# One ring of seven PSUM banks with a new order in the attention, and an own order for its last quad

## The chip, the core and the metric

One core of a Trainium2 chip runs the whole block. Its engines are TensorE (PE, with weight loads PEld), VectorE (DVE), ScalarE (ACT), GpSimd (POOL) and SyncE (SP, which issues DMAs). The metric is device microseconds of one execution.

## The reference

A transformer block with adaptive layer norm. Attention has 32 heads of 18 dimensions and one key/value head for all of them; the MLP has 4608 hidden units. All tensors are float32; x is 2048 x 576.

```python
mod = (_silu(c) @ w_mod).reshape(c.shape[0], 6, 1, -1)
sa, ca, ga, sb, cb, gb = (mod[:, i] for i in range(6))
h = _layernorm(x, axis=-1) * (1 + ca) + sa
x = x + ga * _A_ref(h, A_wq, A_wk, A_wv, A_wo)
h = _layernorm(x, axis=-1) * (1 + cb) + sb
x = x + gb * _B_ref(h, B_w1, B_b1, B_w2, B_b2)

# _A_ref: multi-query attention
scores = jnp.einsum("bhqd,bkd->bhqk", q, k) * (Dh ** -0.5)
p = _softmax(scores, axis=-1)
o = jnp.einsum("bhqk,bkd->bhqd", p, v)
```

## The kernel before

Three stages follow one another. Stage 1 (to about 134 us) makes layer norm, projections and the first maxima. Stage 2 (134 to 1374 us) is the attention. Stage 3 is the MLP. Only stage 2 and its seam to stage 3 are touched.

**Quads.** The attention runs over 32 quads: four blocks of 512 queries (`tb`) by eight groups of four heads. In quad n the engine PE works through a written list of tokens: `QUAD` for n = 0 to 8, `QUADW` for n = 9 to 30, and a list built from `LAST` and `LASTW` for n = 31. PE executes in this order and cannot pass a waiting instruction.

- `S0`, `S1`: a score matmul (`st_mm`, L931): 128 keys by 512 queries of one head, contraction over 64 rows, row group 0 or 1 of the array. ACT takes its exp into a P tile (L933). A quad has 64. There are four P tiles (`bufs=4`), each for 128 keys (`kc`), so four score matmuls fill one.
- `M0`, `M1`: a maxima matmul for the next quad (L319): 128 queries by 512 keys. DVE reduces it to one maximum per query (L953). A quad has 48.
- `X1`, `R1`: eight pairs per quad that get the last two key blocks with one reduction: ACT takes the Relu of a matmul with key differences (L941, L944), and DVE combines it with a second matmul (L319, L951).
- `Vk`: P·V for k quarter blocks of 128 queries (`pv_mm`, L921), four heads side by side in column groups of 32. It lags 8 quarter blocks behind; a quad has 64. The sum of a quad stands in the bank `psC`.
- `WO`: one of 24 pieces of the output product (`wo_next`, L723), 14 matmuls of 288 columns for 128 rows of an earlier block, added to x by DVE (L727). In some quads it is followed by two transposes of a layer-norm tile (L155), which also take a bank each.
- `T1 RC T2 OS`: the rest of the quad before (`post_quad`): transpose on DVE (L741), reciprocal and product (L744, L745), transpose back (L747), and split into two parts `os` (L757, L758), which DMAs on SP put in place. `F1 F2` finish the maxima. `RW` reloads a part of the output weights.

**Banks.** PSUM has eight banks. Before, scores, X, WO and small products take the next of four banks `psB`, maxima the next of three `psM`, and `psC` has one. In quad 31, and at the end of quad 30, where no maxima are left, every second score takes a `psM`. A matmul waits until the engine that reads the bank's former content is done.

**Quad 30** has one more `WO` at its end. In **quad 31** the list gives a V4 after every four scores, and one `WO` in the middle.

**The seam.** After the last P·V, ACT copies `psC` to O. PE then runs `wo_tile(t, 0, KD - 1)` for tiles t = 0, 1, 2 of the last block (24 matmuls each), which needs nothing of the last quad, while ACT and DVE do the last `post_quad` with `form` steps for the MLP between (L1049, L1056, L1058; `todo`, L1082). Then `wo_tile(t, KD - 1, KD)` adds the last part to tiles 0 to 2, and tile 3 (`rest`) is done between the first MLP products. Tiles 0, 1 and 3 use `psA` (two buffers), tile 2 two `psB`.

Of the kernel before, what the change touches and what calls it, by code (L numbers as in the profile page):

```python
# [32 lines left out]
def block_kernel(ctx: ExitStack, tc, x, wqkv, wo, w1, b1, w2, b2, c, wmod, ident_in, out):  # L33
# [850 lines left out]
    QUAD = """S0 M0 S1 S1 M0 V3 S0 M1 S1 M0 M1 S0 V3 M0 S1 M1 S0 V2 M0 S1 S1 M0 X1 S0 V4 T1 X1 M0 M1 M0 S1 S0
            V4 S1 RC M0 S1 S0 M0 S0 M1 V3 S0 M1 R1 S1 S0 M0 X1 V3 M0 S1 S1 R1 S0 M0 S1 V3 M0 X1 M0 S0 S1 S0
            M1 V3 M0 S1 S1 M0 S0 R1 S0 V3 R1 S0 S1 M1 S0 M0 X1 V3 M0 S1 M0 S1 S0 S0 R1 V3 M0 X1 S0 M1 S0 M1
            V3 S1 M0 M0 S1 T2 S0 S1 V4 M0 S1 S0 M1 S0 M1 V3 S0 R1 S1 M0 F1 S1 S0 V3 X1 M0 S1 M0 R1 S0 F2 OS
            V4 M0 M1 S0 S1 M0 X1 V4 S1 M0 S1 S0 M1 M0 S1 V2 R1 S0 M1 S0 V2 S0 S1 M0 M1 V2 S1""".split()
# [616 lines left out]
```

## Time and profile before

| | us |
|---|---|
| median of 3 runs | 2227.75 |
| lowest, highest | 2227.24, 2228.18 |
| span of the profiled execution | 2225.7 |
| PE busy | 2207.4 |
| DVE busy | 1931.9 |
| ACT busy | 1639.8 |
| POOL busy | 1527.0 |

The span runs from the first to the last instruction of the profiled execution; the device time of a run has about 2 us around it. Busy time of PE counts a matmul from start to its modelled end, with waits of the pipeline in it. Where this document gives a time of day, it is in us from the start of that span. A quad is measured from one O copy (L738) to the next.

### The profile page before, as it was taken

How to read it: one execution, taken by the hardware profiler on the slowest of the kernel's cores; microseconds unless marked ns; L12 is line 12 of the kernel's file. 1: busy time of each engine (PE TensorE's matmuls, PEld its weight loads, DVE VectorE, ACT ScalarE, POOL GpSimd, SP SyncE). 2: the span in 40 equal slices, each digit the busy share in tenths (PEclk: the TensorE clock that was granted, in tenths of full speed). 3: DMA queues.
4: the chain of work that ended last, by engine and by line, in shares of the span. 5: the costliest groups of instructions: out<-in, count | busy, mean ns of one | idle time of the engine just before them, and what ended most of it. 6: DMA issues, size and time to landing. Idle time of an engine off the chain costs nothing.

```text
span 2225.7 us, 46108 instructions
## 1 busy us (share of the span) xinstructions
PE 2207.4 (99%) x16630; PEld 1451.2 (65%) x16630; DVE 1931.9 (87%) x3415; ACT 1639.8 (74%) x3145; POOL 1527.0 (69%) x1761
## 2 busy tenths in 40 slices
PE   8999999999999999999999999999999999999999
PEld 6654544444544445454454545888888898989898
DVE  7589999999999999999999983887888878888887
ACT  5569999999999999999999997444444444343443
POOL 6653455666776687677676631888888867877776
PEclk9999999999999999999999999999999999999999
DMA  6232143433333333333333322666666646676664
GB/s 231 85 131 92 34 135 115 139 125 119 127 119 114 115 129 105 107 126 111 126 123 117 115 70 63 205 178 175 178 179 180 185 129 182 180 218 188 177 185 124
DMA packets 184776, 308.00 MB, mean 138 GB/s; under 512 B 19711, under 2 KB 75407, under 8 KB 184549
## 3 DMA queue, kind: packets, MB, share of 16 engines
q1 hardware_dynamic: 184405, 304.91, 44.3%
q8 instruction: 132, 2.16, 0.4%
q14 instruction: 95, 0.78, 0.1%
q10 hardware_dynamic: 144, 0.15, 0.0%
HBM read 200.97 MB, written 93.79 MB: 132 GB/s over the span
## 4 chain that ended last, share of the span: by engine, by line
PE 93%; ACT 1%; DVE 1%; issue 0%; ACTq 0%; DVEq 0%
PE psC L921 24%; PE psB L1144 18%; PE psA L1247 16%; PE psB L931 14%; PE psM L319 12%; PE psB L723 2%; PE psB L941 2%; PE psA L1281 1%; PE psA L723 1%; ACT P L933 1%; PE psB L155 0%; PE psB L248 0%; PE psB L357 0%; PE psM L931 0%; DVE mx L344 0%; DVE mx L337 0%
## 5 line engine op out<-in xcount | busy, mean ns | idle before, releaser
L933 ACT ACTIVATE P<-psB 128x512 f32<-128x512 f32 x2008 | 1051.1, 621 | 43.8 <-PE psM L319 20.0
L953 DVE TENSOR_REDUCE mx<-psM 128x1 f32<-128x512 f32 x1476 | 934.3, 682 | 29.9 <-PE psM L319 12.9
L931 PE MATMUL psB<-qst,KS 64*128 64x512 f32 x2008 | 603.5, 435 | 0.1
L319 PE MATMUL psM<-KS,qst 64*128 64x512 f32 x1722 | 591.2, 435 | 0.5 <-DVE mx L337 0.5
L921 PE MATMUL psC<-P,V 128*32 128x256 f32 (+3 forms) x6600 | 571.9, 440 | 0.5 <-ACT O L738 0.5
L931 PEld LDWEIGHTS psB<-qst,KS 64*128 64x128 f32 x2008 | 300.4, 184 | 225.6 <-ACT P L933 185.1
L319 PEld LDWEIGHTS psM<-KS,qst 64*128 64x128 f32 x1722 | 284.1, 184 | 185.6 <-DVE mx L953 130.2
L1144 PE MATMUL psB<-ops,w1a 128*128 128x512 f32 x1512 | 393.8, 396 | 0.2 <-DVE h L1159 0.2
L1144 PEld LDWEIGHTS psB<-ops,w1a 128*128 128x128 f32 x1512 | 270.1, 188 | 46.7 <-DVE h L1159 0.6
L921 PEld LDWEIGHTS psC<-P,V 128*32 128x32 f32 x6600 | 146.4, 108 | 185.3 <-issue 156.6
L1253 DVE TENSOR_TENSOR XT<-psA,XT 128x576 f32<-128x576 f32 x330 | 241.8, 753 | 18.6 <-PE psA L1247 13.2
L1247 PEld LDWEIGHTS psA<-w2s,big 128*128 128x128 f32 x1584 | 223.0, 188 | 14.0 <-POOL big L1221 2.5
L1247 PE MATMUL psA<-w2s,big 128*128 128x288 f32 x1584 | 230.5, 294 | 0.0
L1157 ACT ACTIVATE psB<-gs 128x512 f32<-128x512 f32 x144 | 86.7, 602 | 127.8 <-DVE gs L1156 127.7
L1221 POOL TENSOR_TENSOR big<-s,big 128x512 fp32r<-128x512 f32 x132 | 170.8, 1294 | 10.6
L951 DVE CUSTOM_DVE_ANT_0 xc<-psM,xc 128x512 f32<-128x512 f32 x246 | 166.3, 683 | 12.8 <-PE psB L931 6.4
L1153 ACT ACTIVATE h<-psB,b1t 128x512 f32<-128x512 f32 x144 | 97.9, 680 | 102.0 <-PE psB L1144 81.3
L758 POOL TENSOR_TENSOR os<-O,os 128x512 fp32r<-128x512 f32 x31 | 39.9, 1286 | 185.4 <-ACT os L757 185.4
L944 ACT ACTIVATE xc<-psB 128x512 f32<-128x512 f32 x246 | 154.7, 629 | 4.0 <-PE psB L941 1.4
L1156 DVE SCALAR_TENSOR_TENSOR gs<-psB,h 128x512 f32<-128x512 f32 x144 | 98.6, 685 | 39.8 <-ACT psB L1154 39.7
L792 POOL TENSOR_TENSOR r<-r,r 128x256 fp32r<-128x256 f32 (+1 forms) x162 | 121.8, 752 | 13.0
L1162 ACT ACTIVATE big<-h 128x512 fp32r<-128x512 f32 x39 | 24.7, 634 | 133.8 <-DVE h L1159 133.8
(212 smaller groups left out, 3326.8 us busy)
## 6 DMA issues: line engine op xcount, KB each, us to landing
w1a<-w1scr SPq DMA_DIRECT2D x252, 256.0 KB
w2s<-w2sum SPq DMA_DIRECT2D x132, 288.0 KB
w1scr<-r SPq DMA_DIRECT2D x126, 256.0 KB
w2s<-w2scr SPq DMA_DIRECT2D x76, 288.0 KB
w2scr<-r SPq DMA_DIRECT2D x72, 288.0 KB
w2sum<-r SPq DMA_DIRECT2D x72, 288.0 KB
qst<-qscr SPq DMA_DIRECT2D x192, 72.0 KB
w1a<-w2scr SPq DMA_DIRECT2D x33, 288.0 KB
```

Of the source, the lines that this page charges most:

```text
L319: pe.matmul(o, QST[n][64 * g:64 * g + 64, p, 128 * qt:128 * (qt + 1)], KS[64 * g:64 * g + 64, 512 * kb:512 * (kb + 1)], start=True, stop=True)
L792: po.tensor_tensor(o[:, n:2 * n], src, o[:, :n].bitcast(F32), op=ALU.subtract)
L921: pe.matmul(PVt[n][32 * j:32 * (j + 1), cs], V[:, kc, :], t[:, j, cs], start=(kc == 0 and h0 == 0), stop=(kc == 15), skip_group_check=True)
L931: pe.matmul(t, KS[64 * g:64 * g + 64, 128 * kc:128 * (kc + 1)], QST[n][64 * g:64 * g + 64, i, :], start=True, stop=True)
L933: ac.activation(P[n, kc][:, 2 * i + g, :], t, AF.Exp, scale=SCALE)
L944: ac.activation(XC[-1], t, AF.Relu)
L951: ve.tensor_tensor_reduce(c, t, c, 1.0, -3.0e38, ALU.add, ALU.max, o)
L953: ve.tensor_reduce(o, t, axis=AX.X, op=ALU.max)
L1144: pe.matmul(o, x, y, start=(first and i == 0), stop=(i == len(terms) - 1), skip_group_check=True)
L1221: po.tensor_tensor(unit(u, 1), x, unit(u, 0).bitcast(F32), op=ALU.subtract)
L1247: pe.matmul(p[:, i, :288], x[:, ts_], W2S[k][:, y], start=(bool(first) and q == 0), stop=(q == 2), skip_group_check=True)
L1253: ve.tensor_tensor(o, p[:, :, :288], o, op=ALU.add)
```

## The change

The seven banks besides `psC` become one ring, from which each token takes the bank that was taken longest ago; each `+` behind a token skips one. All of the stage's users take from it. `QUAD` keeps its sequence and gets `+` marks; `QUADW` is a new sequence with marks. Quad 30 loses its extra `WO`. Quad 31 has a list of its own (`LAST`): P·V in runs of 8 to 12 quarter blocks, two `WO`, and two `WP`: the first 12 matmuls of the output product of tile 2 of the last block, one half each, added to x at once. So the seam runs only tiles 0 and 1 ahead, tile 2 starts at its last part (`first=KD - 1`), and the `form` steps stand behind most of the last `post_quad`.

```diff
-    def psB(): return PS["t"].tile([128, 512], F32, name="psB", bufs=PS["b"])
+    def psB(): return bank() if RING else PS["t"].tile([128, 512], F32, name="psB", bufs=PS["b"])
+    RING = []
+    def bank(rank=0):
+        b = RING.pop(rank)
+        RING.append(b)
+        return PS["t"].tile([128, 512], F32, name="bk%d" % b, bufs=1)
...
     open_ps("2", 4)
-    psM(), psC()
+    RING.extend(range(3))
+    bank(), bank(), bank(), psC()
+    RING[:] = 3, 0, 4, 1, 5, 2, 6
...
-    def wo_mm(tb, t, h2, p, k0, k1):
+    def wo_mm(tb, t, h2, p, k0, k1, end=KD, first=0):
...
-                pe.matmul(p[:, :288], a, b, start=(k == 0 and i == 0), stop=(k == KD - 1 and i == len(terms) - 1))
+                pe.matmul(p[:, :288], a, b, start=(k == first and i == 0), stop=(k == end - 1 and i == len(terms) - 1))
...
-    QUAD = """S0 M0 S1 S1 M0 V3 S0 M1 S1 M0 M1 S0 V3 M0 S1 M1 S0 V2 M0 S1 S1 M0 X1 S0 V4 T1 X1 M0 M1 M0 S1 S0
...
-    QUADW = """M1 M1 S0 S0 X1 S1 M0 V4 S1 M0 S1 S0 M1 M0 V4 M0 S1 S0 M0 S1 T1 M0 X1 V4 S1 RC S0 S0 M1 M0 S1 V4
-            S0 R1 M1 S0 S1 M0 S1 V3 S1 M0 S0 X1 M0 M0 S1 V2 M0 S1 S0 R1 V2 M0 X1 M0 S1 S0 S1 M0 V4 S0 T2 R1
-            M0 S1 OS S0 M1 WO S0 R1 M1 S0 M1 S0 X1 V3 S0 M1 M0 S1 S1 M1 S0 V3 M0 S1 S0 R1 S0 M0 X1 V3 M0 S1
-            X1 M0 S1 M0 S1 V4 S1 M0 R1 S0 M1 S0 V4 S0 M1 M0 F1 S1 S0 S1 V4 M0 S1 M0 X1 S0 M1 F2 V4 M1 S0 S0
-            S1 M0 S1 M0 V3 R1 S0 S0 S1 R1 M0 V3 S0 S1 M0 S1 M0 S1 V3 M0 S1 M1 S0 M1 S0 V3""".split()
-    LASTW = "S0 S1 S0 S1 S0 S1 WO V4 S0 S1 V4".split()
-    LAST = "S0 S1 S0 S1 V4 S0 S1 S0 S1 V4".split()
+    QUAD = """S0+ M0 S1 S1+ M0 V3 S0 M1 S1+ M0 M1++ S0 V3 M0 S1+ M1 S0+ V2 M0 S1+ S1 M0+ X1 S0+ V4 T1 X1 M0 M1 M0
...
+    QUADW = """S1+ M0 M0 X1 S0 X1 M0 V3 S1 M0 M0+ S1 R1 S0+ V2 M1 S0 M0 S1+ S0 R1+ V3 M0 X1+ S0 S1+ S0+ M1 V4 S0 T1
+            M1+ S0 S1 M0 S1+ V4 S1 M0 M1 S0 S1+ M0 V4 S1 M0 S1 S0+ M1 S0 R1 V4 S1 M0 M0 RC X1+ S0 M1+ S1 V3 S0
+            M1 S1+ S0 M0 S1 M0 V3 R1 S1 M0 M1+ S0 S1+ S0 V4 S1 T2 OS M0 X1++ M0 S1+ M0 WO S0 M1 S0 M1 S0 M1 V3
+            S1 S0 M1 S0 M0 X1 V3 S1 M0 M1+ M0 S1+ S0 V4 M0 S1+ S0 S1 S0+ R1+ M0 V4 S0+ S1 M0 M1++ M1 S0+ V3 S0
+            R1 M0+ F1 S1 S0 X1+ V4 M0 S1 M0 S1+ S0+ M1 F2 V3 S0+ R1 S0+ S1 M0 S1 M0 V3 M0 X1 S1 M0+ S1 R1+ S0 V3""".split()
+    LAST = """S1 S0 S1 S0 V8 S0 S1 T1 RC S0 S1 T2 S0 S1 WO S0 S1 S0 S1 OS S1 S0 V9 S1 S0 S1 S0 S1 S0 S1 V11 S0 S1
+            S0 S1 S0 S1 WO RW S0 S1 S0 S1 S0 S1 S0 V10 S1 S0 S1 S0 S1 S0 V2 S0 S1 S0 S1 S0 S1 WP V8 S0 S1 S1 S0
+            S1 S0 V8 S1 S0 S1 S0 S0 S1 WP S0 S1 S0 S1 V12""".split()
...
-            if n == NQT - 2:
-                order = order + ["WO"]
         else:
-            order = []
-            for d in range(8):
-                order += LASTW + ["RW"] if d == 4 else LAST
-                order += {1: ["T1"], 2: ["RC"], 4: ["T2"], 5: ["OS", "V4"]}.get(d, [])
+            order = LAST
...
+            elif tok == "WP":
+                h2 = part.popleft()
+                p = psB()
+                wo_mm(NB - 1, 2, h2, p, 0, KD - 1, KD - 1)
+                wo_add(NB - 1, 2, h2, p)
...
+    RING.clear()
     open_ps("3", 4)
...
-            wo_mm(NB - 1, t, h2, wop[t][0][h2], k0, k1)
+            wo_mm(NB - 1, t, h2, wop[t][0][h2], k0, k1, first=KD - 1 if t == 2 else 0)
...
-    for t in range(3):
+    for t in range(2):
         wo_tile(t, 0, KD - 1)
-    todo = deque(("+B11 +T2", "-B11 =T3 +B21 +T3", "-T2 -T3", "-B21"))
+    todo = deque(("+B11 +T2", "", "", "-B11", "-T2", "=T3 +T3 -T3 +B21 -B21"))
```

## Rows read from the trace of the kernel before

**Rows 1.** The page, its part 1: busy us, share of the span, instructions.
```profile
PE 2207.4 (99%) x16630; PEld 1451.2 (65%) x16630; DVE 1931.9 (87%) x3415; ACT 1639.8 (74%) x3145; POOL 1527.0 (69%) x1761
```
**Rows 2.** Windows: us, busy of PE PEld DVE ACT POOL, clock, DMA, GB/s.
```profile
323.43:360.81 37.38, 37.38 (x363) 18.51 (x362) 36.52 (x71) 36.98 (x77) 26.73 (x40) 1.00 0.41 138
789.17:828.45 39.28, 39.28 (x345) 19.21 (x345) 37.91 (x75) 37.33 (x77) 33.76 (x47) 1.00 0.43 144
```
**Rows 3.** Timeline of weight loads: start, us, engine, line, out<-in, count, idle before.
```profile
796.85 0.18 PEld L319 LDWEIGHTS psM<-KS,qst 64*128 64x128 f32 x1 [0.20 <-issue]
...
797.51 0.16 PEld L921 LDWEIGHTS psC<-P,V 128*32 128x32 f32 x8 [0.31 <-issue]
798.08 0.18 PEld L319 LDWEIGHTS psM<-KS,qst 64*128 64x128 f32 x1 [0.41 <-issue]
...
805.18 0.18 PEld L931 LDWEIGHTS psB<-qst,KS 64*128 64x128 f32 x1 [0.41 <-ACT P L933]
...
806.30 0.59 PEld L921 LDWEIGHTS psC<-P,V 128*32 128x32 f32 x16 [0.28 <-issue]
807.09 0.18 PEld L319 LDWEIGHTS psM<-KS,qst 64*128 64x128 f32 x1 [0.20 <-DVE mx L953]
...
810.21 0.16 PEld L921 LDWEIGHTS psC<-P,V 128*32 128x32 f32 x8 [0.24 <-issue]
811.21 0.18 PEld L931 LDWEIGHTS psB<-qst,KS 64*128 64x128 f32 x1 [0.84 <-ACT P L933]
...
812.11 0.16 PEld L921 LDWEIGHTS psC<-P,V 128*32 128x32 f32 x8 [0.36 <-issue]
```
**Rows 4.** The same timeline, around a WO piece.
```profile
801.14 1.88 PEld L723 LDWEIGHTS psB<-wos,big 126*128 126x128 f32 x14 [0.34 <-ACT P L933]
803.19 0.18 PEld L931 LDWEIGHTS psB<-qst,KS 64*128 64x128 f32 x1 [0.17 <-issue]
```
**Rows 5.** Waits, 173.0 to 1302.57: who waited for whom: us, times, longest.
```profile
PEld psB L931 <- ACT P L933: 174.3, 301, 0.8
...
PEld psM L319 <- DVE mx L953: 123.3, 229, 0.8
```
**Rows 6.** Timelines of ACT (quad 31) and DVE (a QUADW quad).
```profile
1346.57 1.30 ACT L933 ACTIVATE P<-psB 128x512 f32<-128x512 f32 x2
1347.52 1.32 ACT L933 ACTIVATE P<-psM 128x512 f32<-128x512 f32 x2
...
798.68 1.88 DVE L953 TENSOR_REDUCE mx<-psM 128x1 f32<-128x512 f32 x3
800.48 0.45 DVE L147 BATCH_NORM_STATS2 bst<-Z 128x6 f32<-128x288 f32 x1
```
**Rows 7.** Timeline, the end of quad 30 and the start of 31.
```profile
1335.87 1.89 PEld L723 LDWEIGHTS psB<-wos,big 126*128 126x128 f32 x14 [0.62 <-issue]
...
1336.59 0.75 ACT L933 ACTIVATE P<-psM 128x512 f32<-128x512 f32 x1
1337.92 0.19 PEld L931 LDWEIGHTS psB<-qst,KS 64*128 64x128 f32 x2 [0.16 <-issue]
...
1338.45 1.09 ACT L933 ACTIVATE P<-psB 128x512 f32<-128x512 f32 x2 [1.11 <-PE psB L931]
```
**Rows 8.** Timeline, the seam from the attention to the MLP.
```profile
1373.82 6.41 PEld L723 LDWEIGHTS psA<-wos,big 126*128 126x128 f32 x48 [0.84 <-issue]
...
1373.99 0.60 ACT L738 ACTIVATE O<-psC 128x512 f32<-128x512 f32 x1 [1.20 <-PE psC L921]
...
1375.57 1.23 DVE L1058 TENSOR_TENSOR ops<-yr,ops 128x1024 fp32r<-128x1024 f32 x1 [0.24 <-ACT ops L1056]
...
1382.87 0.68 DVE L758 TENSOR_TENSOR big<-O,big 128x512 fp32r<-128x512 f32 x1
...
1384.49 1.55 DVE L1078 TENSOR_TENSOR XT<-psA,XT 128x576 f32<-128x576 f32 x2 [0.35 <-PE psA L723]
...
1387.06 1.75 PEld L723 LDWEIGHTS psA<-wos,big 126*128 126x128 f32 x12
```

More of the change, by code (lines that the diff above doesn't have):

```diff
@@ L353, in smax_fin1, with smax_fin2 @@
             ve.tensor_reduce(m[:, 8:], mm[:, 8:, :3], axis=AX.X, op=ALU.max)
-    def smax_fin2(n):
-        p = psB()
+    def smax_fin2(n, rank=0):
+        p = bank(rank) if RING else psB()
         pe.transpose(p[:16, :128], MR.pop(n), ident)
@@ L883, in block_kernel @@
     LAG = 8
-    QUAD = """S0 M0 S1 S1 M0 V3 S0 M1 S1 M0 M1 S0 V3 M0 S1 M1 S0 V2 M0 S1 S1 M0 X1 S0 V4 T1 X1 M0 M1 M0 S1 S0
[L885 to L888, printed above, removed]
@@ L894, in block_kernel @@
-    LASTW = "S0 S1 S0 S1 S0 S1 WO V4 S0 S1 V4".split()
-    LAST = "S0 S1 S0 S1 V4 S0 S1 S0 S1 V4".split()
+    QUAD = """S0+ M0 S1 S1+ M0 V3 S0 M1 S1+ M0 M1++ S0 V3 M0 S1+ M1 S0+ V2 M0 S1+ S1 M0+ X1 S0+ V4 T1 X1 M0 M1 M0
+            S1 S0 V4 S1 RC M0+ S1 S0 M0+ S0+ M1 V3 S0 M1 R1 S1+ S0 M0+ X1 V3 M0 S1 S1+ R1 S0 M0 S1 V3 M0+ X1 M0
+            S0 S1 S0 M1 V3 M0+ S1 S1+ M0 S0 R1+ S0 V3 R1+ S0 S1 M1 S0 M0 X1 V3 M0+ S1 M0 S1 S0 S0 R1 V3 M0+ X1
+            S0+ M1 S0 M1+ V3 S1 M0+ M0 S1 T2 S0 S1 V4 M0 S1 S0 M1+ S0 M1 V3 S0 R1+ S1 M0 F1 S1 S0 V3 X1 M0 S1 M0
+            R1 S0 F2 OS V4 M0+ M1 S0+ S1 M0+ X1 V4 S1 M0 S1+ S0 M1 M0+ S1 V2 R1 S0 M1 S0+ V2 S0 S1 M0 M1 V2 S1""".split()
@@ L925, in pv_mm, with st_mm @@
             next(posts[0])
-    def st_mm(n, kc, g, i, ps):
+    def st_mm(n, kc, g, i, rank):
         if (n, kc) not in P:
             P[n, kc] = pb.tile([128, 4, TB], F32, name="P", bufs=4)
-        t = ps()
+        t = bank(rank)
         pe.matmul(t, KS[64 * g:64 * g + 64, 128 * kc:128 * (kc + 1)], QST[n][64 * g:64 * g + 64, i, :],
@@ L935, in block_kernel, with mx_mm @@
     XC = deque()
-    def mx_mm(n, u, kb, what, g):
+    def mx_mm(n, u, kb, what, g, rank):
         p, qt = UNITS[u]
         if what == "X":
-            t = psB()
+            t = bank(rank)
             pe.matmul(t, QST[n][64 * g:64 * g + 64, p, 128 * qt:128 * (qt + 1)], KD1[64 * g:64 * g + 64, :],
@@ L945, in mx_mm @@
             return
-        t = psM()
+        t = bank(rank)
         o = mx_tile(n)[:, 8 * g + 4 * p + qt, (2 if what == "R" else kb):][:, :1]
@@ L968, in block_kernel, with wo_next @@
     pieces = deque((tb, t, h2) for tb in range(NB - 1) for t in range(NT) for h2 in range(2))
-    def wo_next(ps):
+    def wo_next(rank):
         tb, t, h2 = pieces.popleft()
-        wo_piece(tb, t, h2, ps())
+        wo_piece(tb, t, h2, bank(rank))
         for _ in range(2):
@@ L977, in wo_next @@
             fill.append(ln2_rows(tb, t))
+    part = deque((0, 1))
     pq = 0
@@ L983, in block_kernel @@
             order = QUADW if n > NQ else QUAD
-            if n == NQT - 2:
-                order = order + ["WO"]
-        else:
-            order = []
-            for d in range(8):
-                order += LASTW + ["RW"] if d == 4 else LAST
-                order += {1: ["T1"], 2: ["RC"], 4: ["T2"], 5: ["OS", "V4"]}.get(d, [])
+        else:
+            order = LAST
         if n < NQT - 1:
-            kf, kr = (sum(int(tok[1]) for tok in order[:order.index(a)] if tok[0] == "V") // 4 for a in ("F2", "RC"))
+            names = [tok[:2] for tok in order]
+            kf, kr = (sum(int(tok[1]) for tok in order[:names.index(a)] if tok[0] == "V") // 4 for a in ("F2", "RC"))
             quiet = kf - 2, kf - 1, kr - 1
         for tok in order:
+            rank = tok.count("+")
+            tok = tok.rstrip("+")
             if tok[0] == "V":
-                g = int(tok[1])
+                g = int(tok[1:])
                 while g:
@@ L1005, in block_kernel @@
                 g = int(tok[1])
-                st_mm(n, ns[g] // 2, g, ns[g] % 2, psM if ns[g] % 2 and (n == NQT - 1 or n == NQT - 2 and ns[g] > 24) else psB)
+                st_mm(n, ns[g] // 2, g, ns[g] % 2, rank)
                 ns[g] += 1
@@ L1010, in block_kernel @@
                 if unit:
-                    mx_mm(*unit, tok[0], int(tok[1]))
+                    mx_mm(*unit, tok[0], int(tok[1]), rank)
             elif tok == "WO":
-                wo_next(psB)
+                wo_next(rank)
+            elif tok == "WP":
[3 more added lines that the diff above has]
+                wo_add(NB - 1, 2, h2, p)
             elif tok == "RW":
@@ L1017, in block_kernel @@
             elif tok[0] == "F":
-                (smax_fin1 if tok == "F1" else smax_fin2)(n + 1)
+                smax_fin1(n + 1) if tok == "F1" else smax_fin2(n + 1, rank)
             elif n:
```

## The prediction

> **What bounds the kernel now.** The page's busy line comes first: PE 99% [rows 1]. A busy PE may be a waiting one, so the stage table is next: attention quads of 37.38 us (QUAD order) and 39.28 us (QUADW), in which DVE is busy 36.52 and 37.91, ACT 36.98 and 37.33 [rows 2]. Three engines are all within 1 to 2 us of the quad. Which one sets it is seen in the weight loads of one QUADW quad, read as alternating runs: a run of P·V (K=128 in four 32-column tiles) and a run of score and maxima matmuls (64-row tiles in pairs, S, M, R, X) [rows 3]. From first load to the next run's first load, V2, V3, V4 take 0.57, 0.78, 1.00 us: 0.215 per 128 query columns plus about 0.15 for the change. Score runs of 4, 6 and 7 take 0.66, 0.90, 1.12: about 0.22 per pair plus 0.23. One change to P·V and back thus costs some 0.38 us, and a seventh matmul costs a whole pair. WO takes 2.05 [rows 4].
> Adding these for a quad of before. QUAD: P·V 12x0.78+5x1.00+4x0.57=16.6; score runs 8x1.12+10x0.90+3x0.66=19.9; sum 36.5 of 37.38. QUADW: P·V 9x1.00+8x0.78+2x0.57=16.4; score runs 10x1.12+9x0.90+0.66=20.0; WO 2.05; sum 38.4 of 39.28. So PE's own order is 98% of a quad; only about 0.85 us of each is PE held by something else. The waits view does name ACT and DVE for 174 and 123 us [rows 5], but most of that is gap under a running P·V (the 0.84 at 811.21 [rows 3] ends a V4 of its normal 1.00).
> This is why the rule "changing tiling mode drains the TensorE" (the Trainium skill, TensorEngine Tiling (Array Packing), Key Properties) fits: the trace puts 0.38 us on a pair of such changes; the page gives no figure.
>
> **QUAD (9 quads): same order, new banks.** The tokens are unchanged in sequence; only which of seven banks each takes differs. A score run of six or seven needs nearly all seven banks, and P·V begins when the last of them has been freed, whoever holds it. A score that takes a DVE bank early leaves an ACT bank for the maxima behind it; the run ends with the same release. I take -0.05 a quad, -0.5 in all; ends: all of the 0.85 gone (-7.7), or twice it (+7.7), the second only if a run ends on a bank freed later.
>
> **QUADW (quads 9 to 29, 21 of them): new order.** V runs are 8 V4, 10 V3, 1 V2: 8.00+7.80+0.57=16.4, as before, again 19 of them. Score runs become 8 of seven and 12 of six instead of 10, 9 and one of four: 8x1.12+12x0.90=19.8 against 20.0. That is -0.2 a quad, -4.2 in 21. The other 0.85 can move either way. ACT does 72 evacuations at 0.475 (two in 0.95) and DVE 56 at about 0.6 (three in 1.88) [rows 6], so a run of seven with its V3 (1.90) asks ACT for four (1.90) and DVE for three (1.80): nothing in the count gets easier. I take -0.1 a quad for a better sequence around WO, where ACT and DVE must be stocked for 2.05 us: -2.1. Ends: -0.65 a quad (-14) and +0.7 (+15). Sum taken -6.3.
>
> **Quad 30: its extra WO goes.** It stood at the end, where maxima have run out: PE is held for 2.05 us (1335.87 to 1337.92), ACT runs dry for 1.11 [rows 7]. Without it the next scores come 2.05 earlier, but ACT still has the queue it had, so ACT gains the 1.11 only, with the order's own 0.2 for this quad: -1.3 (ends -2.05 and 0).
>
> **The last quad.** Before, from its first score load (1337.92 [rows 7]) to the first tail load (1373.82 [rows 8]) it takes 35.9. ACT: 64 exps x 0.475 plus O and `os`, taken at 0.5 each, are 31.4; the rest is start (0.5), a dry spell behind WO, and at the end 1.2 in which O waits for the last P·V [rows 8].
> After: PE has eight P·V runs of 72 quarter blocks in all (8, 9, 11, 10, 2, 8, 8 and 12 with the last 4): 72x0.215+8x0.15=16.7; score runs 2x1.12+7x0.90+2x0.66=9.9; two WO of about 1.9 and two WP (12 of 14 matmuls) of 1.6: 7.0. Sum 33.6, against 30 before, so PE and ACT are level. Walking the order with seven banks: ACT starts 1.4 late (it drains quad 30 until 1337.34, and scores come from 1335.87 on [rows 7]), keeps busy over the first WO, V9, V11 and V10, and runs dry only across "WP V8" (1.6+1.85 against six exps, 2.85): about 0.9. At the end V12 hides the last exps. 1.4+31.4+0.9+last P·V and hand-over 1.6 = 35.3; with some bank waits 35.6. So -0.3, ends -1.5 and +2.5. What moves with it: OS puts ACT behind DVE's transpose, with seven scores queued behind it; between O and OS there are ten exps (4.75), and the four steps that OS needs (two transposes, reciprocal, POOL's product) take some 3 by estimate. On SP, OS and then RW stand ahead of the w1 loads; RW waits for the second WO, some 20 us before the tail needs either.
>
> **The tail.** Tile 2's first 24 matmuls leave it: a tile pair of 48 loads takes 6.41 [rows 8], so -3.2 on PE. Cover: before, O to the last `os` part took 9.5 us (1373.99 to 1383.55 [rows 8]) while PE ran 72 products. Without the forms between, T, R, product, transpose, one form (1.23), `os` take about 4.8; PE's 48 products (6.4) still cover it, so PE has no hole there. But the same forms now come after: DVE has about 9.5 us of the same work plus some 1.2 of waiting for ACT's copies, so the adds of tiles 0 and 1, which before waited for PE (0.35 at 1384.49 [rows 8]), come at about 1385.3 on the old clock, 0.9 late. Tile 3 needs a `psA` that they free: it starts at 1386.1 in place of 1387.06 [rows 8]. So -0.9 of the 3.2 is kept (ends -3.2 and 0).
>
> **Sum.** -0.5-6.3-1.3-0.3-0.9 = -9.3 on this execution (span 2225.7, 2.1 below the median 2227.75): span 2216.4, time **2218.5**.
>
> **Rivals.**
> (1) The waits go, too. For: 0.85 us a quad is there to take, and a ring lets either kind of matmul use any free bank. Against: a run ends with its last bank. Price: 0.5 more in 30 quads, -15: 2204, with most of that, 2207.
> (2) Order and banks are neutral: the sequence is no better and the 0.2 is eaten by waits. For: PE's sum differs by 0.5%. Only quad 30, last quad and tail are left: -2.5: 2225.
> (3) Slower: banks tie ACT and DVE together. Following the tokens, 28 of 73 ACT-bound matmuls of a QUADW quad take a bank that DVE held last, and 28 of 56 DVE-bound ones an ACT bank. Every second quad DVE also does layer-norm steps (0.45 for the sums of one half tile [rows 6]) and two transposes take two more banks out of turn; a score then waits for a late reduce while ACT runs dry. Price: +0.7 a quad in 21 = +14.7 in place of -2.1, with the rest +7.5: 2235. It decides the sign from about +0.34 a quad ((4.2+3.0)/21).
> (4) The granted clock. It is 1.00 (2.4 GHz) in the quads shown [rows 2], in which matmuls already cycle through seven banks behind ACT and DVE. At 1.2 GHz the streaming part of a quad (16x0.85+68x0.22=28.6) would take as much again; three such quads make +86: 2304.
> A page speaks for (4): the Trainium skill, TensorE: Matmul & The Clock Gate, "A second HAM failure mode: psum-queue depth-cycling", where matmuls cycling through PSUM banks make the clock swing. This trace, doing that, shows no fall.
>
> **How the numbers follow.** Forecast (2213 to 2223.2) 0.48; (1) 0.20; (2) 0.20; (3) 0.10; (4) 0.02. About 0.2% (4.5 us) is what a measurement of this kernel can tell from no change, so faster begins at 2223.3: forecast and (1), and a little of (2), give 0.70; same 0.19; slower 0.11. The range leaves out the far end of (1) and (3) with (4): 2206 to 2228.
>
> **What would show it.** Right: QUAD quads at 37.3 to 37.4 from O copy to O copy; QUADW at 38.8 to 39.1; no change in the length of V runs; the last quad within 1.5 us of 35.9 with ACT dry once, behind "WP V8"; the adds of the tail with no wait for PE, and PE waiting for them before tile 3. Wrong: QUADW below 38.6 or above 39.6, score runs with waits in their middle behind an engine that doesn't evacuate them, a last quad over 38 us, PE idle before the tail's last products.

## The result and the profile after

| | before | after |
|---|---|---|
| median of 5 runs each | 2227.75 | 2238.47 |
| lowest, highest | 2227.20, 2229.87 | 2237.92, 2241.12 |
| span of the profiled execution | 2225.7 | 2238.8 |

The ratio is 1.005 (95% interval 1.0039 to 1.0061): the change costs 10.7 us where 9.3 less were predicted, and the time lies outside the range. The profiled execution of after took 2240.68, 2.2 above the median, so sums made on it come to 13.1, not 10.7. The mean granted clock was 0.995 in the two executions above 2240 and 0.996 or 0.997 in the other three.

The page of after: part 1 (answers to [rows 1]), the shares by engine of the chain that ended last (part 4), and the row of the score matmuls in part 5 (busy, mean ns, idle before and its releaser).

```profile
PE 2205.1 (98%) x16822; PEld 1459.5 (65%) x16822; DVE 1929.4 (86%) x3417; ACT 1646.2 (74%) x3145; POOL 1527.2 (68%) x1761
...
PE 88%; DVE 3%; POOL 2%; DMA 1%; ACT 1%; issue 1%; SPq 0%; DVEq 0%; POOLq 0%; ACTq 0%
...
L942 PE MATMUL bk<-qst,KS 64*128 64x512 f32 x2048 | 598.4, 433 | 12.0 <-DMA qst<-ms 9.7
```

The busy line says almost nothing: PE is as busy as before, on a span 13 us longer. What is new stands in the other two: a DMA on the chain that ended last, and score matmuls that stood idle 9.7 us for the DMAs `qst<-ms`. These are F2's: four small DMAs on SP that put the maxima of the next quad into two rows of each row group of its queries.

Windows of after (columns as in [rows 2]): one quad in QUAD order, two neighbours in QUADW order.

```profile
323.21:360.67 37.46, 37.46 (x363) 18.96 (x361) 36.52 (x71) 37.04 (x76) 27.25 (x40) 1.00 0.38 129
594.00:634.28 40.29, 40.09 (x358) 19.85 (x358) 37.99 (x77) 38.10 (x77) 23.55 (x34) 1.00 0.29 98
634.28:673.83 39.54, 38.95 (x353) 19.27 (x353) 37.50 (x76) 37.70 (x76) 34.46 (x49) 1.00 0.37 127
```

The same two quads of before:

```profile
590.92:630.84 39.93, 39.93 (x350) 19.77 (x350) 38.01 (x76) 37.87 (x77) 25.19 (x34) 1.00 0.27 91
630.84:670.12 39.27, 39.27 (x345) 19.18 (x345) 37.90 (x75) 37.31 (x76) 31.72 (x46) 1.00 0.39 133
```

QUAD is unchanged (37.46 against the 37.38 of [rows 2]). A QUADW quad is 0.3 to 0.4 longer, PE is now idle in it, and the granted clock is 1.00. By O copies, over the whole stage (profiled executions; e7 and e11 are experiments below):

| stretch, us | before | after | e7 | e11 |
|---|---|---|---|---|
| O copies 0 to 7 (QUAD) | 262.83 | 263.04 | 263.06 | 262.77 |
| 7 to 8 (QUADW begins) | 37.24 | 38.57 | 38.55 | 37.24 |
| 8 to 29 (21 QUADW) | 829.52 | 839.31 | 830.60 | 829.53 |
| 29 to 31 (quads 30, 31) | 71.41 | 71.36 | 68.29 | 70.24 |
| last O copy to the end | 851.66 | 854.00 | 853.68 | 848.86 |

The 1.3 between O copies 7 and 8 is no loss of its own: the new QUADW has three P·V runs and three score runs ahead of its O copy where the old had two of each, and the stretch 29 to 31 gets that back. So quads 30 and 31 really cost 1.3 more in after, and 1.8 less in e7.

**Inside a QUADW quad.** The weight loads were split into runs as in [rows 3], each held against the shortest time of its length (0.66, 0.89, 1.11 for score runs of 4, 6, 7; 0.57, 0.78, 1.00 for V2, V3, V4). Means over 20 quads (O copies 9 to 29); WO and its transposes take 2.28 in every kernel:

| us per quad | before | after | e7 | e9 | e2 | e3 | e8 | e1 | e12 |
|---|---|---|---|---|---|---|---|---|---|
| quad | 39.51 | 39.98 | 39.58 | 39.76 | 40.06 | 40.28 | 40.81 | 40.99 | 39.91 |
| score runs, shortest | 19.92 | 19.71 | 19.71 | 19.71 | 19.71 | 19.71 | 19.92 | 19.71 | 19.92 |
| waits in score runs | 0.93 | 1.13 | 1.20 | 1.28 | 1.65 | 1.46 | 2.22 | 2.14 | 1.32 |
| P·V runs with the wait behind | 16.39 | 16.86 | 16.40 | 16.50 | 16.42 | 16.83 | 16.39 | 16.86 | 16.39 |

The new order is 0.21 shorter, as predicted. It loses 0.20 in score runs and 0.47 behind P·V runs; nearly all of the latter stands behind one run, the V3 ahead of the next quad's first score, which takes 1.25 on average in place of 0.78.

That place in one quad of after, in its timelines (weight loads PEld, matmuls PE, DMA issues SPq; start, us, engine, line, out<-in, idle before):

```profile
583.00 0.09 PEld L365 LDWEIGHTS bk<-ident,mxf 128*16 128x16 f32 x1 [0.37 <-ACT xc L955]
584.39 2.83 SPq L372 DMA_DIRECT2D qst<-ms  x4
587.10 0.16 PEld L932 LDWEIGHTS psC<-P,V 128*32 128x32 f32 x8 [0.27 <-issue]
588.47 0.18 PEld L942 LDWEIGHTS bk<-qst,KS 64*128 64x128 f32 x1 [1.21 <-ACT P L944]
588.50 0.46 PE L942 MATMUL bk<-qst,KS 64*128 64x512 f32 x1 [0.54 <-DMA qst<-ms]
```

And in the same quad of before (an S0 comes first there, at 586.89, the first S1 at 587.38):

```profile
578.37 0.09 PEld L357 LDWEIGHTS psB<-ident,mxf 128*16 128x16 f32 x1 [0.35 <-ACT P L933]
579.78 2.87 SPq L364 DMA_DIRECT2D qst<-ms  x4
586.89 0.18 PEld L931 LDWEIGHTS psB<-qst,KS 64*128 64x128 f32 x1
587.38 0.18 PEld L931 LDWEIGHTS psB<-qst,KS 64*128 64x128 f32 x1 [0.20 <-ACT P L933]
```

F2's transpose (L365) is loaded at 583.00, the four DMAs are issued from 584.39 on, one behind the other in 2.83 us, and the first score starts at 588.47, 5.47 behind the transpose. Before, it had 8.5. In 19 of the 21 quads 10 to 30 of after the load of the first score starts 4.03 to 4.17 behind the first of the four issues; before it started 7.11 to 7.23 behind. The new QUADW puts F2 three P·V runs ahead of the quad's end where the old had five, and its first score is an S1, whose two DMAs are issued last. A reader should note the two names: the weight load at 588.47 names ACT, long done, since a wait for several semaphores is put down to one of them; the matmul row names the DMA.

The seam and the start of quad 31, in the timelines of PE and DVE and in windows of after:

```profile
1346.93 0.82 PE L942 MATMUL bk<-qst,KS 64*128 64x512 f32 x4 [1.72 <-DMA qst<-ms]
1347.68 3.19 PE L932 MATMUL psC<-P,V 128*32 128x512 f32 x16
...
1393.12 3.58 DVE L1073 TENSOR_TENSOR ops<-yr,ops 128x1024 fp32r<-128x1024 f32 x2 [1.13 <-ACT ops L1071]
1396.62 1.14 DVE L1073 TENSOR_TENSOR opt<-yr,opt 128x512 fp32r<-128x512 f32 x1
1397.69 1.41 DVE L1094 TENSOR_TENSOR XT<-psA,XT 128x576 f32<-128x576 f32 x2
1398.49 2.52 PE L733 MATMUL psA<-wos,big 126*128 126x288 f32 x12 [3.49 <-DVE XT L1094]
```
```profile
1348.20:1351.60 3.40, 3.40 (x20) 1.01 (x14) 0.00 (x0) 1.90 (x4) 0.00 (x0) 0.50 0.00 0
1399.40:1402.81 3.41, 3.41 (x13) 3.02 (x12) 3.38 (x5) 0.56 (x1) 0.00 (x0) 0.50 0.00 0
```

PE waits 1.72 for F2's DMAs ahead of quad 31 and 3.49 for the adds ahead of tile 3, and behind each wait the granted clock is 0.50 (1.2 GHz) for 3.4 us. Before had neither wait [rows 7, rows 8]. The fall does not follow such a wait in every execution: e4 and e5 below have the same waits with the clock at 1.00.

### The profile page after: what moved, and what is told of

Same layout as the page of the kernel before. It is cut to its first block, busy times and chain, and to the rows that moved or that the text cites. A ratio compares the mean times of both kernels' runs of the same rounds, so it can differ in the third digit from the quotient of the medians.

```text
span 2238.8 us, 46467 instructions
## 1 busy us (share of the span) xinstructions
PE 2205.1 (98%) x16822; PEld 1459.5 (65%) x16822; DVE 1929.4 (86%) x3417; ACT 1646.2 (74%) x3145; POOL 1527.2 (68%) x1761
## 4 chain that ended last, share of the span: by engine, by line
PE 88%; DVE 3%; POOL 2%; DMA 1%; ACT 1%; issue 1%; SPq 0%; DVEq 0%; POOLq 0%; ACTq 0%
PE psC L932 22%; PE psB L1160 18%; PE psA L1263 16%; PE bk L942 15%; PE bk L327 10%; PE bk L733 2%; PE bk L952 2%; PE psA L1297 1%; DMA qst<-ms 1%; DVE mx L964 1%; POOL r L802 0%; PE psB L256 0%; DVE ops L1073 0%; POOL r L863 0%; PE bk L365 0%
## 5 line engine op out<-in xcount | busy, mean ns | idle before, releaser
L944 ACT ACTIVATE P<-bk 128x512 f32<-128x512 f32 x2048 | 1066.9, 623 | 45.0 <-PE bk L327 19.3
L964 DVE TENSOR_REDUCE mx<-bk 128x1 f32<-128x512 f32 x1476 | 935.1, 682 | 52.9 <-PE bk L327 41.4
L942 PE MATMUL bk<-qst,KS 64*128 64x512 f32 x2048 | 598.4, 433 | 12.0 <-DMA qst<-ms 9.7
L327 PE MATMUL bk<-KS,qst 64*128 64x512 f32 x1722 | 591.5, 438 | 0.8
L942 PEld LDWEIGHTS bk<-qst,KS 64*128 64x128 f32 x2048 | 297.2, 185 | 279.1 <-ACT P L944 155.5
L327 PEld LDWEIGHTS bk<-KS,qst 64*128 64x128 f32 x1722 | 272.9, 185 | 130.0 <-ACT P L944 59.1
L932 PEld LDWEIGHTS psC<-P,V 128*32 128x32 f32 x6792 | 153.3, 108 | 193.5 <-issue 160.9
L962 DVE CUSTOM_DVE_ANT_0 xc<-bk,xc 128x512 f32<-128x512 f32 x246 | 167.3, 680 | 2.9 <-PE bk L327 1.7
L955 ACT ACTIVATE xc<-bk 128x512 f32<-128x512 f32 x246 | 151.7, 617 | 1.3 <-PE bk L327 1.3
```

Of the source, the lines that this page charges most:

```text
L327: pe.matmul(o, QST[n][64 * g:64 * g + 64, p, 128 * qt:128 * (qt + 1)], KS[64 * g:64 * g + 64, 512 * kb:512 * (kb + 1)], start=True, stop=True)
L932: pe.matmul(PVt[n][32 * j:32 * (j + 1), cs], V[:, kc, :], t[:, j, cs], start=(kc == 0 and h0 == 0), stop=(kc == 15), skip_group_check=True)
L962: ve.tensor_tensor_reduce(c, t, c, 1.0, -3.0e38, ALU.add, ALU.max, o)
L964: ve.tensor_reduce(o, t, axis=AX.X, op=ALU.max)
```

## The experiments

Each time is a median, its ratio against runs of the kernel before on the same chip. Theory S: the new QUADW order loses; rivals: the banks (B), the last quad (L), the DMAs (D).

**e1. The new order on the old banks.** Before, with the new QUADW without its marks.

```diff
-    QUADW = """M1 M1 S0 S0 X1 S1 M0 V4 ...
+    QUADW = """S1 M0 M0 X1 S0 X1 M0 V3 ...
```

> The kernel before with one edit: the new QUADW sequence, without marks, on the old four and three banks; quad 30 keeps its extra WO, quad 31 and the seam are as before. Theory S (the loss sits in the sequence: the rows of F2 land after the next quad asks for them, and OS stands too close behind RC): quads 9 to 29 take as long as in the changed kernel, 39.5 to 40.5 us, some 0.4 to 0.6 more than before, so about +10, 2237 to 2239. Rival B (the ring ties ACT and DVE together): without the ring the quads return to 39.0 to 39.9, and the time is 2222 to 2228.

Measured 2261.55, 1.015 (1.0135 to 1.0165), above both ranges. On the old banks the order loses more than it does in the ring: beside the same 0.47 behind P·V, 2.14 us a quad are waited in score runs. So the ring with its marks repairs a part of what the order costs, and rival B's idea that this order loses by the ring falls.

**e2. F2 one run earlier.** After, with the run `S0+ S1 M0 M1++ M1 S0+ V3` moved from ahead of F2 to behind it.

```diff
-  ... S0+ S1 M0 M1++ M1 S0+ V3 S0 R1 M0+ F1 ... M1 F2 V3 S0+ R1 ...
+  ... S0 R1 M0+ F1 ... M1 F2 V3 S0+ S1 M0 M1++ M1 S0+ V3 S0+ R1 ...
```

> The changed kernel with one block of QUADW moved: S0 S1 M0 M1 M1 S0 V3 goes from before the block of F1 to behind F2, so F2 and its four DMAs come about 1.7 us earlier. Theory S: the wait for the rows of F2 at the start of the next quad (0.5 to 0.6 in most QUADW quads, 1.7 before quad 31) goes, -10 to -13, 2226 to 2228; the fall of the clock after the 1.7 goes with it. Rival B: nothing but noise, within 2 us of 2238.5.

Measured 2239.81, 1.0055 (1.0038 to 1.0071). The wait behind P·V is gone (16.42), yet the quad is no shorter: score runs wait 0.52 more. Most of it stands in the moved run itself (0.90 in after, 1.25 here), which asks DVE for three maxima in a row and now follows F2 (timeline of weight loads of e2):

```profile
582.07 0.19 PEld L327 LDWEIGHTS bk<-KS,qst 64*128 64x128 f32 x1
582.54 0.29 PEld L327 LDWEIGHTS bk<-KS,qst 64*128 64x128 f32 x2 [0.28 <-DVE mx L964]
```

Moving a run also changes which bank each token meets, so this run could not say what the DMA wait alone is worth. e7 was made for that.

**e3. The chain behind WO.** Three quads of after (from O copies 10, 16 and 22) are 1 us longer than their like. In the first two the run behind WO takes 1.99 and 1.87 in place of 0.89; in the third it takes 1.18, and the V3 ahead of the next quad 2.04. POOL's product comes late, DVE's transpose waits for it, and ACT, whose `os` stands right behind, is held with the scores queued after it. Timelines of POOL, DVE and ACT of after:

```profile
808.28 1.05 POOL L755 TENSOR_TENSOR T<-T,R 128x512 f32<-128x512 f32 x1
...
809.37 0.71 DVE L757 STREAM_TRANSPOSE O<-T 128x512 f32<-128x512 f32 x1 [0.98 <-POOL T L755]
...
810.11 0.63 ACT L767 ACTIVATE os<-O 128x512 fp32r<-128x512 f32 x1 [1.45 <-DMA w2scr<-r]
```

The row of `os` names a DMA, but `os` starts just behind the end of the transpose (809.37 + 0.71).

e3 puts RC two runs earlier and OS behind WO.

```diff
-  ... S1 M0 M0 RC X1+ ... S1 T2 OS M0 X1++ M0 S1+ M0 WO S0 M1 S0 M1 ...
+  ... RC M1 S0 S1+ M0 V4 ... S1 T2 M0 X1++ M0 S1+ M0 WO S0 M1 OS S0 M1 ...
```

> The changed kernel with RC two runs of P.V earlier in QUADW and OS three tokens behind WO in place of ahead of it. Theory S: the three quads of 40.5 us (POOL late with the product, DVE's transpose and ACT's os wait for it) come down to 39.5: -3 in all, a little more if ACT also waits briefly in the other quads: 2233 to 2236. Rival B: the waits behind WO stay, as they come from banks, 2238.

Measured 2246.19, 1.0086 (1.0071 to 1.0102), above both expectations. The three long quads are gone, and every other one is longer: a run of SSMSMX behind OS now waits 0.46 in each. Three quads with 1 us each were not worth a step that is met in every quad.

**e4. The adds first.** After, with the seam's adds of tiles 0 and 1 ahead of the MLP's T3 and B21 forms and t0.

```diff
-    todo = deque(("+B11 +T2", "", "", "-B11", "-T2", "=T3 +T3 -T3 +B21 -B21"))
+    todo = deque(("+B11 +T2", "", "", "-B11", "-T2 =T3", "+T3 -T3 +B21 -B21"))
...
+    form(todo.popleft())
+    for t in range(3):
+        wo_tile(t, KD - 1, KD)
     for w in todo:
         form(w)
```

> The changed kernel with the last output products and their adds ahead of the form steps T3, B21 and t0 in the seam. If PE's 3.5 us of idle time in the seam is DVE's order, and the fall of the clock behind it its consequence: -3.5 and up to -1.7 more, 2233.5 to 2235. If DVE is merely full, the wait moves to the next products and the time stays within 1 us of 2238.5.

Measured 2235.32, 1.0035 (1.0022 to 1.0048), 3.15 below after. Timelines of DVE and PE and a window of e4: the adds stand ahead of the long forms, PE goes into tile 3 without a wait, and the clock stays.

```profile
1388.48 1.55 DVE L1094 TENSOR_TENSOR XT<-psA,XT 128x576 f32<-128x576 f32 x2
...
1390.68 3.42 DVE L1073 TENSOR_TENSOR ops<-yr,ops 128x1024 fp32r<-128x1024 f32 x2
...
1391.28 1.76 PE L733 MATMUL psA<-wos,big 126*128 126x288 f32 x12
```
```profile
1391.50:1396.50 5.00, 5.00 (x33) 4.64 (x32) 4.96 (x5) 0.00 (x0) 2.51 (x1) 1.00 0.35 103
```

The last O copy to the end takes 849.40, against 851.66 of before and 854.00 of after. Ahead of quad 31, where e4 is as after, the wait is the same, but the clock stays (timeline of PE and a window of e4):

```profile
1344.83 0.83 PE L942 MATMUL bk<-qst,KS 64*128 64x512 f32 x4 [1.72 <-DMA qst<-ms]
```
```profile
1343.00:1352.00 9.00, 7.28 (x54) 4.05 (x54) 2.02 (x4) 7.64 (x17) 1.05 (x1) 1.00 0.01 1
```

So its stretch from O copy 29 to 31 is 69.88, and of after's 71.36 about 1.5 is the fall of the clock.

**e5 and e6. The last quad and the seam alone,** in the kernel before, on its 4 + 3 banks; e6 with the adds first as in e4.

```diff
             if n == NQT - 2:
-                order = order + ["WO"]
...
-                order += LASTW + ["RW"] if d == 4 else LAST
+            order = LAST
```

> The kernel before with the changed last quad, the extra WO of quad 30 taken out and the changed seam alone; banks and both quad orders as before. Theory S (the loss is the new QUADW order): 2227.75, less 0.1 for quads 30 and 31, plus the 2.3 by which the stretch behind the last O copy grew: 2230 (2228 to 2232), with PE's 3.5 us wait for the adds ahead of tile 3 and the granted clock down behind it, and QUADW quads at 39.25 and 39.9 as before. Theory L (the last quad loses much of the 10.7 us by itself): over 2234.

> As e5, with the adds of tiles 0 and 1 ahead of the late steps of the MLP's forms, as in e4. Theory S: e4 lay 3.2 us below the kernel after, so 2230 - 3.2 = 2226.8 (2225 to 2229), no wait of PE over 1 us behind the last O copy. Theory L: over 2231.

Measured: e5 2234.58, 1.0034 (1.0022 to 1.0046); e6 2228.61, 1.0004 (0.9995 to 1.0013). QUADW is as before in both (829.6 for the 21), which fits S. So the loss in those quads is not the last quad's. But e5 is 4.6 over what S said, on L's side, and e6 near the upper end of S's range: quads 30 and 31 take 75.26 and 73.69 on two classes of banks, against 71.41 of before. The new list alternates P·V runs of 8 to 12 with short score runs; with every second score tied to `psM`, three scores there that ACT has not read hold up the next one (0.98 in the rows below). In the seam e5 waits 3.48 ahead of tile 3 as after does, but its clock stays at 1.00, and the last O copy to the end takes 852.45. The two kernels also show the clock ahead of tile 2. The same score, the same wait, and behind it the first half of tile 2 (timelines of PE, e5 and then e6):

```profile
1363.62 0.50 PE L932 MATMUL psM<-qst,KS 64*128 64x512 f32 x1 [0.98 <-ACT P L934]
1364.05 2.57 PE L723 MATMUL psB<-wos,big 126*128 126x288 f32 x12
```
```profile
1360.70 0.50 PE L932 MATMUL psM<-qst,KS 64*128 64x512 f32 x1 [0.98 <-ACT P L934]
1361.13 1.84 PE L723 MATMUL psB<-wos,big 126*128 126x288 f32 x12
```

From that score to the second P·V run behind it, in windows of e5 and then of e6:

```profile
1363.62:1370.15 6.53, 6.53 (x36) 3.45 (x36) 0.46 (x1) 2.70 (x6) 0.00 (x0) 0.74 0.02 6
```
```profile
1360.70:1365.65 4.95, 4.95 (x36) 2.70 (x36) 0.46 (x1) 2.70 (x6) 0.00 (x0) 1.00 0.03 11
```

The same work at a granted clock of 0.74 and of 1.00: 1.6 us, the difference of their quads 31.

**e7. Nothing waits for F2's DMAs.** After, with the DMAs going to a scratch place; order, banks and count of DMAs kept. The exp leaves the maximum out.

```diff
+                if 0 < n:
+                    sy.dma_start(msdump[2 * g + s], ms[8 * g:8 * (g + 1), s].bitcast(F32))
+                    continue
...
-        ac.activation(P[n, kc][:, 2 * i + g, :], t, AF.Exp, scale=SCALE)
+        ac.activation(P[n, kc][:, 2 * i + g, :], t, AF.Exp, scale=SCALE if n == 0 else SCALE / 32)
```

> The kernel after, with F2's four DMAs of each quad but the first written to a scratch place in DRAM, so that no score waits for them; order, banks and the number of DMAs stay. It leaves the subtraction of the maximum out of the exp (with a smaller scale, so that the values stay finite). Theory D (these DMAs are the loss): the waits behind P·V runs are 0.51 us in a QUADW quad of after against 0.04 of before; 0.47 x 21 = 9.9 us go: 2228.6 (2226 to 2231), QUADW quads at 39.2 and 39.8. Theory B (the time comes back as waits for banks, as it did in e2): no V run is held, but score runs are, 2235 to 2240.

Measured 2228.41, 1.0003 (0.9994 to 1.0012): 10.1 below after. The same two quads as above, in windows of e7, and the place ahead of the first score in its timelines of SP and PE:

```profile
593.39:633.49 40.10, 40.00 (x358) 19.75 (x358) 38.00 (x77) 38.09 (x77) 22.14 (x31) 1.00 0.28 94
633.49:672.76 39.27, 39.27 (x353) 19.40 (x353) 37.55 (x76) 37.57 (x77) 35.19 (x50) 1.00 0.38 130
```
```profile
584.29 1.35 SPq L372 DMA_DIRECT2D msdump<-ms  x4
...
586.99 0.85 PE L936 MATMUL psC<-P,V 128*32 128x384 f32 x8
587.77 0.50 PE L946 MATMUL bk<-qst,KS 64*128 64x512 f32 x1
```

The score follows the V3 in 0.78 with no wait. P·V runs are back at 16.40, score runs wait only 0.07 more than in after, and 8.7 us go in the 21 quads, 3.1 in quads 30 and 31 (the 1.72 and the slow clock behind it). Theory D holds: this wait is the loss. The DMAs to the scratch place also take less time to issue (1.35 for four in place of 2.83), so that SP comes sooner to its next ones; in the QUADW stretch of after no row names a wait of PE for any other DMA. What is left of the new order is nothing: 0.21 shorter, 0.27 more waits than before.

**e8. The old order in the ring,** without marks.

```diff
-    QUADW = """S1+ M0 M0 X1 S0 X1 M0 V3 ...
+    QUADW = """M1 M1 S0 S0 X1 S1 M0 V4 ...
```

> The kernel after with the old QUADW sequence and no marks in it: each token takes the bank that was taken longest ago. Last quad and seam as in the change. Theory S (only the sequence loses): QUADW at 39.25 and 39.9 as before, 2238.5 - 9.8 = 2228.7 (2227 to 2231). Theory B (which bank a token gets sets the waits, and no sequence runs well on banks that weren't chosen for it): waits for ACT and DVE in score runs grow by 0.3 to 1 us a quad: 2235 to 2250.

Measured 2255.36, 1.0124 (1.0109 to 1.014): far from S's 2228.7, and above B's range of 2235 to 2250, too. Waits of the QUADW stretch in e8:

```profile
PEld bk L942 <- DVE mx L964: 86.9, 145, 0.8
PEld bk L327 <- DVE mx L964: 58.7, 101, 0.8
PEld bk L942 <- ACT P L944: 56.1, 83, 0.8
PEld bk L327 <- ACT P L944: 47.4, 134, 0.8
```

On two classes [rows 5] a score waits for ACT and a maxima matmul for DVE. Here scores wait 86.9 us for DVE's reduces and maxima 47.4 for exps, and 1.3 us a quad more are lost in score runs. That is rival (3) of the prediction, at nearly twice its price, but in a kernel without marks. With the marks it is smaller, not gone: in the same stretch of e7 scores wait 46.7 for DVE's reduces and maxima 26.4 for exps. (As in [rows 5], these sums hold gaps under a running P·V, too.)

**e9. The scores last in the first run.** After, every token on its bank.

```diff
-    QUADW = """S1+ M0 M0 X1 S0 X1 M0 V3 S1 M0 M0+ S1 R1 ...
+    QUADW = """M0 X1++ M0+ X1++ M0++ S1 S0 V3 S1+++++ M0 M0 S1 R1++ ...
```

> The kernel after with the first run of QUADW in another order: its two scores stand last in the run (M0 X1 M0 X1 M0 S1 S0 for S1 M0 M0 X1 S0 X1 M0); the marks are worked out anew, so that every token keeps its bank. The first score that needs F2's DMAs is asked for some 0.35 us later in the quad. Theory D (the DMA wait is the loss): of 0.47 us a quad about 0.37 go, 21 x 0.37 = 7.8: 2230.7 (2228.5 to 2233); the wait ahead of quad 31, whose list begins with scores, stays. Theory B (a sequence whose tokens change place loses to bank waits, as in e2 and e8): the V wait goes, score runs wait more, 2235 to 2245.

Measured 2236.14, 1.0035 (1.0022 to 1.0049): 2.3 below after, not 7.8. The 0.37 behind P·V went as expected; 0.2 came back inside the first run (1.38 in place of 1.15). In each of the 20 quads its second X1 now waits 0.29 for DVE ahead of the scores, as in this timeline of weight loads of e9:

```profile
586.80 0.18 PEld L952 LDWEIGHTS bk<-KD,qst 64*128 64x128 f32 x1 [0.29 <-DVE mx L962]
```

**e10. With group 1's DMAs first and the adds first.**

```diff
-        for g in range(2):
+        for g in (1, 0):
             for s in range(2):
                 r = 64 * g + R3 + s
```

> As e9, with F2's DMAs of row group 1 (the group of the first score) issued ahead of those of group 0, and the seam's adds first as in e4. Theory D: the rest of the wait goes too (0.1 x 21 = 2), the wait ahead of quad 31 falls from 1.7 to about 0.3 us and the granted clock stays at 1.00 behind it (some 3 us), and the seam gives 3.2: 2230.7 - 2 - 3 - 3.2 = 2222.5 (2221 to 2226), below the kernel before. Theory B: 2230 and over.

Measured 2230.26, 1.0009 (1.0 to 1.0018), above D's range and just inside B's. Ahead of quad 31 the S1 now waits 0.35, but the S0 behind it, whose DMAs have become the last, waits another 0.85, 1.2 in place of 1.72 (timeline of PE; the second row names ACT, but the load of the S0 starts 4.0 behind the first issue, as a reader of the last DMA does in after):

```profile
1339.16 0.47 PE L942 MATMUL bk<-qst,KS 64*128 64x512 f32 x1 [0.35 <-DMA qst<-ms]
1340.48 0.69 PE L942 MATMUL bk<-qst,KS 64*128 64x512 f32 x3 [0.85 <-ACT P L944]
```

The clock stayed at 1.00. Quads 30 and 31 take 69.65 against 71.38 of e9, most of it the clock's (e4: 69.88 with the whole 1.72), and the seam gave 4.4. QUADW did not move (834.5, e9 834.4): in both kernels the first two scores come 4.34 and 4.46, or 4.65 and 4.75, behind the first issue in all but single quads, later than the 4.03 to 4.17 of after. So the DMAs no longer hold them; what is left is the wait of the first run for DVE (e9). The new order remains 5 us behind the old in its 21 quads.

**e11. The old quads, the new last quad.** Quads 0 to 30 with order and banks of before, quad 31 with the new list in the ring, the adds first.

```diff
+        if OLD:
+            q = OLD["M" if rank == "M" else "B"]
+            b = q.popleft()
+            q.append(b)
+            RING.remove(b)
...
             order = LAST
+            OLD.clear()
```

> The quads 0 to 30 with the order and the 4 + 3 banks of before, quad 31 with the new list in the ring of seven, the seam with its adds first. Theory R (the new last quad pays in the ring, where e5 and e6 had it on 4 + 3 banks and lost 2.3 to 3.9 us in quads 30 and 31): quads 30 and 31 come to 71.4 - 1.8 = 69.6 as e7 had them, the seam gives 2.8: 2227.7 - 4.6 = 2223.1 (2221 to 2225.5). Theory L (the list itself loses, on any banks): quads 30 and 31 at 73 to 75, 2227 to 2230.

Measured 2223.44, 0.9981 (0.9972 to 0.999), inside R's range, the only kernel here below both. Its page, part 1:

```profile
PE 2201.9 (99%) x16646; PEld 1450.1 (65%) x16646; DVE 1931.4 (87%) x3417; ACT 1639.5 (74%) x3145; POOL 1528.3 (69%) x1761
```

1.2 us come from quads 30 and 31 and 2.8 from the seam. On the ring the list takes 70.24, on 4 + 3 banks 73.69 (e6): 3.5 us for the banks alone.

**e12. F2 later in the kernel before.** Two runs later, all else in place.

```diff
-  ... M1 F2 V4 M1 S0 S0 S1 M0 S1 M0 V3 R1 S0 S0 S1 R1 M0 V3 ...
+  ... M1 V4 M1 S0 S0 S1 M0 S1 M0 V3 R1 S0 S0 S1 R1 M0 F2 V3 ...
```

> The kernel before with F2 two runs later in QUADW (behind R1 S0 S0 S1 R1 M0 instead of ahead of V4 M1 S0 S0 S1 M0 S1 M0); all else in place. Theory D: in the kernel after, the first score follows F2's transposition by 5.5 us, of which the DMAs are the end; in before that score came 8.5 us behind F2 and waited for none. F2 two runs later leaves 8.5 - 3.8 = 4.7, so 0.8 us is waited in each of the 22 QUADW quads: some 15 us more (11 to 18), 2239 to 2246, all of it behind the P·V run that stands ahead of the quad's first score. Rival (the place of F2 alone costs nothing; the new order's loss is its own): 2226 to 2231.

Measured 2236.33, 1.0038 (1.0024 to 1.0053): slower by 8.8, below D's range and above the rival's, and not by D's mechanism. P·V runs kept their 16.39. The first score of the old order is an S0, whose DMAs are issued first; it came 4.97 behind F2's load, the S1 5.43, just the 5.47 of after, and neither waited for long. The bound of 5.5 held for group 1 only. The loss is in the score run behind F2 (1.23 in place of 0.90), where the last score wants F2's bank, which two engines have to read. Waits of the QUADW stretch and the timeline of weight loads of e12:

```profile
PEld psB L931 <- DVE ms L360: 5.7, 20, 0.3
```
```profile
583.98 0.18 PEld L319 LDWEIGHTS psM<-KS,qst 64*128 64x128 f32 x1
584.46 0.18 PEld L931 LDWEIGHTS psB<-qst,KS 64*128 64x128 f32 x1 [0.30 <-DVE ms L360]
```

## Why the prediction was wrong

**QUAD** was right: neutral (+0.2 in seven quads).

**QUADW, the order**, was right: -0.21 a quad from run lengths, as summed. No V run and no score run changed its shortest time, so the 0.38 us for a change to P·V and back held. The signs for a QUADW quad were set on one quad of 39.28; before alternates between 39.27 and 39.93, with a mean of 39.51.

**QUADW, the waits**, is the step that failed. The sum took -0.1 a quad, with ends of -0.65 and +0.7, by asking how ACT and DVE keep up. It never asked what else moves with the tokens: F2 moved from five P·V runs ahead of the quad's end to three, with its four DMAs, and the first score changed its row group. The numbers were at hand: 8.5 us from F2 to the first score before, and in the new order 3 x 0.78 + 2 x 1.11 = 4.6, while F2's issue alone ends 4.3 behind its load (579.78 + 2.87 - 578.37). Cost: 0.47 a quad, 10.1 on the median (e7). The upper end taken for the waits, +0.7, did hold the measured +0.67 (0.20 + 0.47), and rival (3) has nearly the time, 2235. That is luck: 0.47 of the 0.67 is a wait for DMAs, of which it does not speak. A bound from the right rows with the wrong mechanism got a chance of 0.10.

The rest of the waits, +0.27 a quad in e7, eats the order's gain: rival (2) describes it. By the means of e7 it stands in two runs. The run behind WO has 0.22 over its shortest time, in the main the chain of e3, whose cure moved the wait to another run. The last run of the quad has 0.20: it takes 1.59 in place of 1.12 in eight of the 20 quads, those in which DVE does layer-norm steps just ahead of it (0.44 at 624.26 in e7), and a maxima matmul then waits for its reduce (0.41 at 626.76). That is the late reduce of rival (3) at a small price; it is read from the trace, and no run took it away alone.

**Quads 30 and 31**: -1.6 was predicted. With no wait for F2's DMAs it is -1.8 (e7, with the 1.3 of the shifted O copy) and -1.2 (e11). That this is near is two errors against each other. In e11 quad 31's first score is loaded at 1333.57 and the first weights of the seam at 1370.22: up to the first of these the time since O copy 29 fell by 2.03 where 1.3 was taken for the WO, and quad 31 took 36.65 where 35.6 was taken and before had 35.90. ACT runs dry once across "WP V8", as foreseen, for 1.28 in place of 0.9. In after the same DMAs cost 3.1 here, since quad 31's list begins with scores: 1.6 for the wait and 1.5 for the clock (e4). That transfers move with the order was missed here, too. That the step depends on the ring, e6 and e11 show: on 4 + 3 banks the same list loses 2.3 to 3.9.

**The seam**: -0.9 was predicted, +2.34 measured. The mechanism stood in the text (the adds late, PE held ahead of tile 3); its size was off twice. The adds were put 11.3 behind the O copy and came 12.85 behind it (1397.69, O at 1384.84): the forms ahead of them were costed at 1.23 and two of them took 3.58. And behind PE's wait of 3.49 the clock was down, 3.4 us at half: some 1.6 more, against e5, which has the wait without the fall. e4 puts the adds first and keeps 2.3 of the 3.2.

**Rival (4)**, the granted clock: it did fall, but behind waits and not from bank cycling (1.00 in all windows of QUAD and QUADW quads above). The page cited for it (the Trainium skill, TensorE: Matmul & The Clock Gate, "A second HAM failure mode: psum-queue depth-cycling") is borne out by no run here. The section ahead of it (the Trainium skill, TensorE: Matmul & The Clock Gate, "HAM oscillation — how this bites in real kernels") speaks of waits for DMA that bring the clock down. The traces agree in part: behind the 1.72 ahead of quad 31 the clock stood at 0.50 for 3.4 us in after, and at 1.00 in e4.

## What to carry to other kernels

When an order is changed, list for every moved step the transfers it issues and count from the step to their first reader, in the new order's own runs; a reader that changes its row group may need another one of several transfers. A wait that is taken away by moving tokens can come back at their banks (e2, e9), so price a wait by an experiment that keeps order and banks (e7). A ring that any engine may draw from is only as good as its choice: the same order cost 1.3 us a quad more with the oldest bank than with two classes (e8), and a list with long alternating runs gained 3.5 from it (e11 against e6).
